# Attention and memory-augmented attention on one core: first x tiles on two DMA queues, the output bank lent to the first projections, phi's exponentials not put off, the last two head groups in turn

## The chip, the cores and the metric

The kernel runs on one core of a Trainium2 chip. The metric is the device time of one execution in microseconds (us), median of several. A profiled run is one execution with every instruction recorded; its length is called the span. Engines: TensorE (PE in the profile; PEld is its weight load), ScalarE (ACT), VectorE (DVE), GpSimd (POOL), and SyncE (SP), which here only issues DMAs. "SPq" and "ACTq" are the instruction streams of SyncE and ScalarE where they issue a DMA.

## The reference, cut to what matters

Two blocks work on their own inputs and their outputs are joined along the last axis. All inputs are bf16; S = 2048, D = 1024, 32 heads of 32.

```python
# A: plain attention, no mask
q, k, v = split(x @ wqkv)                      # 32 heads
o = softmax(q k^T / sqrt(32)) v                # per head, 2048 x 2048 scores
a = o @ wo
# B: four segments of 512 with a memory
phi = lambda t: where(t > 0, t + 1, exp(t))
for s in range(4):
    a_dot = softmax(causal(q_s k_s^T / sqrt(32))) v_s
    a_mem = (phi(q_s) M) / (phi(q_s) z + 1e-6)
    o_s = sigmoid(beta) * a_mem + (1 - sigmoid(beta)) * a_dot
    M += phi(k_s)^T v_s ;  z += sum(phi(k_s))
b = o @ wo
return concatenate([a, b], -1)
```

## The kernel before

Heads are worked four at a time, a *head group* (8 in A). A *unit* is one group with 256 queries (A) or one group with one segment (B, 32 units). A unit's scores are made in *batches*: 8 matmuls of TensorE fill two pairs of PSUM banks, and ScalarE takes the exponential of each pair (128x1024) into a ring of 20 SBUF slots. (In this kernel the results of matmuls go to PSUM banks; all else on the chip is kept in SBUF.) Later TensorE multiplies these by V and by ones ("PV") into one output bank; the slots then come free, and VectorE divides.

What makes this kernel special is that the order of instructions on each engine is not written down by hand. At build time a planner runs all these processes against *assumed* costs: each request to an engine has a cost and a priority (lower goes first), and whichever is ready in the plan is recorded next. Each engine's program is its list in that order, with semaphores between the lists. So a changed cost or priority can change orders everywhere, and a plan that misjudges costs is only noticed on the chip.

```python
def dve(n, rate=1.0):                      # assumed cost of a VectorE operation, us
    return n / rate / 960 + 0.06
PAIRS = [(0, 1), (2, 3), (4, 5)]           # score banks
OB, SB = 6, 7                              # output bank, side bank (projections, memory)
# ... cut
    def first_x(self):                     # x rows 0..511, transposed on TensorE
        # ... cut
        for t in range(4):
            yield do("SP", lambda e, t=t: e.dma_start(self.XS[:, t, :], self.A_x[0][P * t:P * t + P, :]),
                     w=[("XS", t)], cost=0.1, prio=0, tail=2.5 + 0.7 * t)
        Q.fire("x0")
        # ... 4 x (8 transposes on TensorE, copy on VectorE or ScalarE)
    def rest_x(self):                      # x rows 512..2047, transposed by the DMA
        yield ("ev", "x0")
        for c in range(1, 4):
            src = self.A_x[0][512 * c:512 * c + 512, :]
            yield do("SP", lambda e, c=c, src=src: e.dma_start(self.xA[:, :, 512 * c:512 * c + 512], src, transpose=True),
                     w=[("xA", c, t) for t in range(4)], cost=8.0, prio=1, tail=1.5)
    def b_proj(self, n):                   # K, Q, V of B's unit n
        # ... cut
            d = I - (12, 7, 2)[k]          # due so many batches ahead of the unit's scores
            while self.pos < d - self.ahead:
                yield ("ev", ("pos", d - self.ahead))
    def b_mem(self, n):                    # phi, memory read and update of unit n
        # ... cut
        yield do("ACT", lambda e: e.activation(self.E[:, k0:k1, :], KQ[:, k0:k1, :], ACTF.Exp), r=kq, w=["E"],
                 cost=0.1 + 0.427 * nk, prio=6)          # scores' exponentials have prio 0
    def batches(self):                     # order of the score batches
        # ... cut
        for a in range(2, NG * NQ):        # A's units: group after group
            u = ("A", a // NQ, a % NQ)
            out += [(u, k) for k in range(8)]
            # ... B's units strewn in
    def main(self):
        # ... cut
        self.side = Pool([SB])
        self.obank = Pool([OB])
        # ... cut
        def later():
            yield ("ev", ("xA", 3))        # then B's first weights, B's x, beta
```

## Time and profile before

Median 1254.87 us of 3 runs (1250.74 to 1260.59); the profiled run's span is 1254.4 us.

| engine | busy us | share |
|---|---|---|
| ScalarE | 1128.8 | 90% |
| TensorE | 1081.2 | 86% |
| VectorE | 482.2 | 38% |

ScalarE has the most work, and nothing in the change takes work from it. Its timeline therefore splits the span into four terms that can be compared between kernels: the *head* until the first exponential, the *idle* between the first and the end of the last exponential (the gaps over 0.15 us, which are those that the profile counts), the *work* (the rest of that stretch), and the *tail* after it. Before: 21.9 + 76.9 + 1123.8 + 31.8 = 1254.4.

The list of waits of ScalarE (engine, tile, line, who released it: total us, times, longest), kernel before:

```profile
ACT PT L826 <- PE ps L809: 70.6, 48, 6.3
ACT outsb L971 <- PE ps L965: 19.5, 7, 3.7
ACT gcol L483 <- DMA beta<-in_B_beta_dram: 6.3, 1, 6.3
```

The first line is exponentials waiting for scores (L809), the second is output copies in the tail, the last is the wait for the small vector beta.

The timeline of the head, kernel before (start us, duration us, engine, line, operation, count, and in brackets the idle before it with its releaser):

```profile
3.71 2.04 SPq L512 DMA_DIRECT2D OTA<-in_A_x_dram  x3
8.70 2.74 PE L520 MATMUL ps<-ident,OTA 128*128 128x128 bf16 x24 [3.81 <-DMA OTA<-in_A_x_dram]
12.59 3.60 PE L565 MATMUL ps<-xA,WA 128*32 128x512 bf16 x32 [1.15 <-issue]
17.08 3.61 PE L565 MATMUL ps<-xA,WA 128*32 128x512 bf16 x32 [0.89 <-DVE KA L571]
...
21.93 7.44 ACT L826 ACTIVATE WoB<-ps 128x1024 bf16<-128x1024 f32 x8 [9.44 <-PE ps L809]
50.30 0.21 ACT L483 ACTIVATE gcol<-beta 128x8 f32<-128x8 bf16 x1 [6.27 <-DMA beta<-in_B_beta_dram]
56.75 1.94 ACT L826 ACTIVATE PT<-ps 128x1024 bf16<-128x1024 f32 x2 [6.24 <-PE ps L809]
65.47 3.90 ACT L826 ACTIVATE PT<-ps 128x1024 bf16<-128x1024 f32 x4 [6.27 <-PE ps L809]
74.39 1.94 ACT L826 ACTIVATE PT<-ps 128x1024 bf16<-128x1024 f32 x2 [5.02 <-PE ps L809]
```

Tiles 1 to 3 of x land at 8.7 us, when TensorE starts to transpose them. The projections of K and Q run 32 matmuls in 3.6 us, half the rate of later ones (1.9 us; called "half rate" and "full rate" below), with 0.89 us between them for the copy out of the single side bank. After the first 24 exponentials ScalarE idles four times for 5 to 6 us.

In the middle there are six waits of 3 to 5.7 us. The chain of waits around the one that ends at 930 us, kernel before (start us, us, what):

```profile
922.67 0.70 DVE VT L571
...
923.39 3.74 DMA VB<-VT
...
927.26 0.54 PE ps L897 x16
...
929.03 0.49 DVE tB L946
...
929.57 0.40 PE ps L897 x8
929.97 0.36 PE ps L809 x8
...
930.35 1.94 ACT PT L826 x2
```

Read downward: V of a B unit is copied out, transposed by a DMA, then PV of that unit runs in two halves with VectorE's division between, and only behind these does TensorE reach the next score batch.

The end, chain of waits, kernel before:

```profile
1220.27 0.33 PE ps L809 x8
1220.60 6.16 PE ps L965 x112
...
1227.41 10.14 PE ps L965 x188
...
1241.46 5.89 PE ps L965 x107
...
1247.37 0.69 DVE outsb L971
```

After the last score batch (L809) TensorE still has 26.8 us of work to do, nearly all of it output projection (L965).

### The profile page before, as it was taken

The page shows a single profiled execution, that of the slowest core. Times are in us where ns is not written, and L with a number is a line of the kernel's source. Part 1 is how long each engine was busy: PE and PEld are TensorE (multiplying, and loading weights), DVE is VectorE, ACT ScalarE, POOL GpSimd, SP SyncE. Part 2 cuts the span into 40 slices and gives each one's busy share as a digit, 9 for nine tenths or more (in the row PEclk, how much of TensorE's full clock was granted, in tenths as well). Part 3 has the DMA queues.
Part 4 walks back from the last instruction along what each step waited for, and adds up shares of the span by engine and source line. Part 5 has one row for each costly group of instructions (what it writes and reads, how often), then busy time and mean ns, then how long its engine had stood idle before and what let it go on. Part 6 is the DMA issues. An engine that isn't in the chain of part 4 may idle for free.

```text
span 1254.4 us, 49504 instructions
## 1 busy us (share of the span) xinstructions
PE 1081.2 (86%) x23137; PEld 508.4 (41%) x23137; DVE 482.2 (38%) x1065; ACT 1128.8 (90%) x1227; POOL 125.8 (10%) x285
## 2 busy tenths in 40 slices
PE   6588989887889888888899888898888888889997
PEld 2243444443444444443444344343433444434443
DVE  1124333432434444443434444533434436324332
ACT  4469999999999899999999889999987999999981
POOL 1001000100101111111010201110111102100000
PEclk9798999999999999998999999999999999989999
DMA  8422152124212122313121223113122111120112
GB/s 167 86 53 44 36 129 52 37 45 75 52 29 56 40 53 49 57 28 73 44 61 36 48 49 61 36 40 64 38 49 60 33 38 43 32 73 32 37 45 67
DMA packets 214741, 67.23 MB, mean 54 GB/s; under 512 B 203776, under 2 KB 211968, under 8 KB 214528
## 3 DMA queue, kind: packets, MB, share of 16 engines
q1 hardware_dynamic: 214528, 63.99, 23.4%
q8 instruction: 183, 3.00, 1.0%
q14 instruction: 30, 0.25, 0.1%
HBM read 36.70 MB, written 8.39 MB: 36 GB/s over the span
## 4 chain that ended last, share of the span: by engine, by line
ACT 43%; PE 37%; DVE 13%; DMA 2%; issue 2%; SPq 1%; POOL 1%; ACTq 0%
ACT PT L826 42%; PE ps L565 12%; PE ps L897 11%; PE ps L965 7%; PE ps L809 6%; DVE Dt L919 2%; DVE Rb L922 2%; ACT E L670 1%; DVE VT L571 1%; DVE KQB L571 1%; DVE Rall L920 1%; POOL PT L835 1%; DMA beta<-in_B_beta_dram 1%; DVE OTA L926 1%; DVE amem L706 1%
## 5 line engine op out<-in xcount | busy, mean ns | idle before, releaser
L826 ACT ACTIVATE PT<-ps 128x1024 bf16<-128x1024 f32 x1168 | 1086.9, 1067 | 73.0 <-PE ps L809 70.6
L897 PE MATMUL ps<-PT,ones 128*32 128x256 bf16 (+1 forms) x4800 | 298.6, 273 | 0.0
L897 PE MATMUL ps<-PT,VA 128*32 128x256 bf16 x4032 | 256.3, 278 | 33.2 <-ACT PT L826 18.4
L565 PE MATMUL ps<-xA,WA 128*32 128x512 bf16 x3072 | 228.3, 389 | 29.0 <-DVE KQB L571 11.8
L565 PE MATMUL ps<-xB,WB 128*32 128x512 bf16 x3072 | 231.1, 387 | 25.4 <-DVE VT L571 6.7
L809 PE MATMUL ps<-QA,KA 32*128 32x256 bf16 x4096 | 205.8, 275 | 33.0 <-ACT PT L826 26.1
L835 POOL TENSOR_SCALAR_AFFINE_SELECT PT<-PT 128x256 bf16<-128x256 bf16 (+1 forms) x224 | 98.6, 441 | 952.3 <-ACT PT L826 945.9
L897 PEld LDWEIGHTS ps<-PT,VA 128*32 128x32 bf16 x4032 | 108.2, 96 | 132.5 <-ACT PT L826 90.5
L809 PEld LDWEIGHTS ps<-QA,KA 32*128 32x128 bf16 x4096 | 60.9, 92 | 214.5 <-ACT PT L826 172.1
L897 PEld LDWEIGHTS ps<-PT,ones 128*32 128x32 bf16 x4800 | 130.2, 97 | 15.3 <-issue 0.5
L565 PEld LDWEIGHTS ps<-xA,WA 128*32 128x32 bf16 x3072 | 75.5, 97 | 102.6 <-issue 48.6
L565 PEld LDWEIGHTS ps<-xB,WB 128*32 128x32 bf16 x3072 | 77.0, 97 | 94.0 <-issue 70.3
L919 DVE STREAM_TRANSPOSE Dt<-ps 128x256 f32<-128x256 f32 x128 | 57.3, 448 | 147.2 <-PE ps L897 146.5
L571 DVE CAST VT<-ps 128x512 bf16<-128x512 f32 x64 | 43.9, 686 | 139.4 <-PE ps L565 136.6
L571 DVE CAST KQB<-ps 128x512 bf16<-128x512 f32 x64 | 43.8, 685 | 137.2 <-PE ps L565 137.2
L971 DVE CAST outsb<-ps 128x512 bf16<-128x512 f32 x57 | 39.3, 690 | 114.4 <-PE ps L965 114.2
L965 PE MATMUL ps<-WoB,OTB 128*32 128x512 bf16 x1024 | 72.3, 381 | 5.0 <-DVE VT L571 1.9
L965 PE MATMUL ps<-xA,OTA 128*32 128x512 bf16 x1024 | 67.4, 388 | 1.2 <-DVE outsb L971 0.7
L922 DVE STREAM_TRANSPOSE Rb<-Rall 128x256 f32<-128x256 f32 x128 | 56.7, 443 | 3.5
L897 PE MATMUL ps<-PT,VB 128*32 128x256 bf16 (+1 forms) x768 | 46.2, 262 | 10.2 <-DVE tB L946 4.9
L809 PE MATMUL ps<-KQB 32*128 32x128 bf16 (+3 forms) x512 | 44.4, 310 | 5.2 <-ACT PT L826 4.0
L571 DVE CAST QA<-ps 128x512 bf16<-128x512 f32 x32 | 21.8, 683 | 55.1 <-PE ps L565 55.0
(67 smaller groups left out, 463.4 us busy)
## 6 DMA issues: line engine op xcount, KB each, us to landing
WB<-in_B_wk_dram SPq DMA_DIRECT2D x32, 256.0 KB, 2.8
WB<-in_B_wq_dram SPq DMA_DIRECT2D x32, 256.0 KB, 2.9
WB<-in_B_wv_dram SPq DMA_DIRECT2D x32, 256.0 KB, 3.1
out_dram<-outsb SPq DMA_DIRECT2D x64, 128.0 KB, 1.8
WA<-in_A_wqkv_dram SPq DMA_DIRECT2D x24, 256.0 KB, 2.9
WoB<-in_B_wo_dram SPq DMA_DIRECT2D x1, 2048.0 KB, 9.7
xA<-in_A_wo_dram SPq DMA_DIRECT2D x1, 2048.0 KB, 9.6
OTA<-in_A_x_dram SPq DMA_DIRECT2D x4, 256.0 KB, 4.5
```

Source lines behind the costliest of these rows:

```text
L565: ins = e.matmul(self.ps[32 * c:32 * c + 32, bank, :], W[:, i, 32 * c:32 * c + 32], x(i), start=(i == 0), stop=(i == NI - 1))
L571: return e.tensor_copy(dst, self.ps[:, bank, :])
L670: yield do("ACT", lambda e: e.activation(self.E[:, k0:k1, :], KQ[:, k0:k1, :], ACTF.Exp), r=kq, w=["E"], cost=0.1 + 0.427 * nk, prio=6)
L706: yield do("DVE", lambda e: e.scalar_tensor_tensor(self.amem[b][:, :], self.ps[:, bank, :], gA, self.mR[:, :], ALU.mult, ALU.mult), r=[("p ...
L809: ins = e.matmul(self.ps[:, bk, col:col + w], lhs(t, hs), rhs(q0, w, hs), start=True, stop=True)
L826: yield do("ACT", lambda e: e.activation(ap, self.ps[:, pr[0]:pr[1] + 1, :], ACTF.Exp, scale=SCALE), r=[("ps", bk) for bk in pr], w=keys, ...
L835: yield do("POOL", lambda e, m=m, n=n: e.affine_select(m, m, pattern=[[0, n], [1, P]], compare_op=ALU.is_ge, fill=0.0, base=0, channel_mul ...
L897: ins = e.matmul(out, l, r, start=st, stop=sp)
L919: yield do("DVE", lambda e: e.transpose(Dt[:, :], den), r=[("ps", OB)], w=[("Dt", x)], cost=dve(QU), prio=0)
L922: yield do("DVE", lambda e: e.transpose(Rb[:, :].rearrange("p (a b) -> p a b", b=32), self.spread(Rc)), r=[("Rc", ui)], w=[("Rb", x)], cos ...
L965: ins = e.matmul(self.ps[32 * c:32 * c + 32, bank, :], lhs(j)[:, 32 * c:32 * c + 32], W(j), start=(j == 0), stop=(j == NG - 1))
L971: return f(self.outsb[ob][:, :], self.ps[:, bank, :])
```

## The change

By its words: the first x tiles go out on two DMA queues; the output bank is lent to projections until the first PV; phi's exponentials get the highest priority; the last two head groups alternate by query block, so that output rows are finished steadily. The diff holds more: nine warming matmuls at the start, the transposing loads in six pieces, new planner costs, earlier due dates for B's projections, B's first loads (with beta) started at score batch 16, a longer lookahead (`ahead`: a projection may start so many batches before its due date, 12 before and 20 after), and other settings of the planner (the `par` line: B's rate, the order of PV, the dates of B's memory and output). Its core (cuts marked):

```diff
 def dve(n, rate=1.0):
-    return n / rate / 960 + 0.06
+    return n / rate * 0.00088 + (0.14 if rate == 1 else 0.07)
...  (score batch: cost 2 * N256 -> N256; exponential: 0.95 -> 0.9035; DMAs get a bandwidth model)
+    par = dict(b=(18, 14, 10), mem=-2, memM=2, span=66, rate=0.58, ahead=20, sl=4, pv=18, ob=6, lead=4, b0=1, bpos=16, wob=80)
...
+    def warm(self):
+        yield do("DVE", lambda e: e.memset(self.PT[:, 0, :], 0.0), w=[("PT", 0)], cost=0.3, prio=0)
+        # nine 128x512 matmuls of that tile
...
-            yield do("SP", lambda e, t=t: e.dma_start(self.XS[:, t, :], ...
+            Q.spawn(self.load_xs(t, "SP" if t % 2 == 0 else "ACT"))
...
-            d = I - (12, 7, 2)[k]
+            d = I - self.par['b'][k]
...
-                 cost=0.1 + 0.427 * nk, prio=6)
+                 cost=0.093 + 0.427 * nk, prio=-1)
...
+        units = [(a // NQ, a % NQ) for a in range(2, (NG - 2) * NQ)]
+        p = self.par["lead"]
+        units += [(NG - 2, q) for q in range(p)]
+        for q in range(NQ):
+            units += [(NG - 1, q)]
+            if q + p < NQ:
+                units += [(NG - 2, q + p)]
...
-        self.side = Pool([SB])
-        self.obank = Pool([OB])
+        self.side = Pool([SB, OB])
+        self.obank = Pool([])
+        self.first_pv = False
...
-        self.ahead = 12
+        self.ahead = self.par['ahead']
...
         for k in (0, 1, 2):
-            Q.spawn(self.load_WA(k, 0, 0))
+            Q.spawn(self.load_WA(k, 0, 0, "SP" if k == 0 else "ACT"))
...
         def later():
-            yield ("ev", ("xA", 3))
+            yield ("ev", ("pos", self.par["bpos"]))
```

More of the change, by code (lines that the diff above doesn't have):

```diff
@@ L26 @@
 class Op:
-    __slots__ = ("eng", "idx", "fn", "deps", "clock", "inc", "end", "waits", "dma")
+    __slots__ = ("eng", "idx", "fn", "deps", "clock", "inc", "end", "waits", "dma", "ex")
     def __init__(self, eng, idx, fn):
         self.eng, self.idx, self.fn = eng, idx, fn
-        self.deps, self.clock, self.inc, self.end, self.waits, self.dma = [], None, False, 0.0, [], None
+        self.deps, self.clock, self.inc, self.end, self.waits, self.dma, self.ex = [], None, False, 0.0, [], None, eng
 class Recorder:
@@ L66, in deps, with add @@
         return deps
-    def add(self, eng, fn, r, w, order=None):
+    def add(self, eng, fn, r, w, order=None, via="SP"):
         deps = self.deps(eng, r, w, order)
@@ L76, in add @@
             op.dma = c
+            op.ex = via
         else:
@@ L93, in resolve @@
         for op in self.all:
-            ex = "SP" if op.dma is not None else op.eng
+            ex = op.ex
             kn = known[ex]
@@ L125, in play @@
         for op in self.all:
-            if ("SP" if op.dma is not None else op.eng) != name:
+            if op.ex != name:
                 continue
@@ L155 @@
 class Req:
-    __slots__ = ("eng", "fn", "r", "w", "cost", "prio", "mode", "tail", "proc", "seq", "order")
+    __slots__ = ("eng", "fn", "r", "w", "cost", "prio", "mode", "tail", "proc", "seq", "order", "kb")
 class Pool:
@@ L178, in __init__ @@
         self.mode = None
+        self.dma_free = 0.0
         self.events = {}
@@ L277, in dispatch @@
             ready = 0.0
-            for d in self.R.deps(eng, rq.r, rq.w, rq.order):
+            for d in self.R.deps("SP" if rq.kb else eng, rq.r, rq.w, rq.order):
                 if d.end + LAT > ready and d.eng != eng:
@@ L296, in dispatch @@
         assert all(k in self.R.lastw for k in rq.r), rq.r
-        op = self.R.add(eng, rq.fn, rq.r, rq.w, rq.order)
+        op = self.R.add("SP" if rq.kb else eng, rq.fn, rq.r, rq.w, rq.order, eng)
         cost = rq.cost
@@ L305, in dispatch @@
         op.end = start + cost + rq.tail
+        if rq.kb:
+            self.dma_free = max(self.dma_free, start + min(cost, 0.6)) + rq.kb / 230
+            op.end = max(start + cost, self.dma_free) + 1.7
         self.busy[eng] += cost
@@ L321, in run, with do @@
             raise RuntimeError(f"stuck processes: {self.nproc} " + str([k for k, v in self.events.items() if v is not True]))
-def do(eng, fn, r=(), w=(), cost=0.1, prio=5, mode=None, tail=None, order=None):
+def do(eng, fn, r=(), w=(), cost=0.1, prio=5, mode=None, tail=None, order=None, kb=None):
     rq = Req()
-    rq.order = order
+    rq.order, rq.kb = order, kb
     rq.eng, rq.fn, rq.r, rq.w, rq.cost, rq.prio, rq.mode = eng, fn, list(r), list(w), cost, prio, mode
@@ L453, in pkey, with load_WA @@
         return ("WoB", i // 2) if k == 1 else ("OTA", 2 + i // 4, i % 4)
-    def load_WA(self, k, g, prio=5):
+    def load_WA(self, k, g, prio=5, via="SP"):
         col = (1024, 0, 2048)[k] + P * g
         src = self.A_wqkv.rearrange("(i p) n -> p i n", p=P)[:, :, col:col + P]
-        yield do("SP", lambda e: e.dma_start(self.WA[k][:, :, :], src), w=[("WA", k)], cost=0.1, prio=prio, tail=2.8)
+        yield do(via, lambda e: e.dma_start(self.WA[k][:, :, :], src), w=[("WA", k)], cost=0.8, prio=prio, kb=256)
         self.Q.fire(("WA", k, g))
@@ L464, in load_WB @@
         src = self.B_w[k].rearrange("(i p) n -> p i n", p=P)[:, :, P * g:P * g + P]
-        yield do("SP", lambda e: e.dma_start(self.WB[k][:, :, :], src), w=[("WB", k)], cost=0.1, prio=prio, tail=2.8)
+        yield do("SP", lambda e: e.dma_start(self.WB[k][:, :, :], src), w=[("WB", k)], cost=0.6, prio=prio, kb=256)
         self.Q.fire(("WB", k, n))
@@ L469, in load_xB @@
         src = self.B_x[0][512 * s:512 * s + 512, :]
-        yield do("SP", lambda e: e.dma_start(self.xB[:, :, :], src, transpose=True), w=["xB"], cost=8.0, prio=6, tail=2.5)
+        yield do("SP", lambda e: e.dma_start(self.xB[:, :, :], src, transpose=True), w=["xB"], cost=5.2, prio=6, kb=1024)
         self.Q.fire(("xB", s))
@@ L480, in f @@
                     return e.dma_start(self.beta[32 * h:32 * h + 32, 0:NG], src)
-            yield do("SP", f, w=[("beta", h)], cost=0.1, prio=8)
+            yield do("SP", f, w=[("beta", h)], cost=0.5, prio=8, kb=300)
         gA, gB = self.gcol[:, 0, :], self.gcol[:, 1, :]
@@ L504, in constants, with f @@
         yield pool(lambda e: e.memset(self.Mf[:, :, :], 0.0), [("Mf", g) for g in range(NG)], 1.0)
+    def warm(self):
+        yield do("DVE", lambda e: e.memset(self.PT[:, 0, :], 0.0), w=[("PT", 0)], cost=0.3, prio=0)
+        def f(e):
+            for _ in range(9):
+                ins = e.matmul(self.ps[:, SB, :], self.PT[:, 0, 0:P], self.PT[:, 0, :], start=True, stop=True)
+            return ins
+        yield do("PE", f, r=[("PT", 0)], w=[("ps", SB)], cost=3.8, prio=0, mode=FULL)
     def first_x(self):
@@ L511, in first_x @@
         for t in range(4):
-            yield do("SP", lambda e, t=t: e.dma_start(self.XS[:, t, :], self.A_x[0][P * t:P * t + P, :]),
-                     w=[("XS", t)], cost=0.1, prio=0, tail=2.5 + 0.7 * t)
-        Q.fire("x0")
+            Q.spawn(self.load_xs(t, "SP" if t % 2 == 0 else "ACT"))
         for t in range(4):
+            yield ("ev", ("XS", t))
             b = banks[t]
@@ L530, in first_x, with load_xs @@
         Q.give(self.pairs, [(banks[0], banks[1]), (banks[2], banks[3])])
+    def load_xs(self, t, via):
+        yield do(via, lambda e: e.dma_start(self.XS[:, t, :], self.A_x[0][P * t:P * t + P, :]), w=[("XS", t)], cost=0.5, prio=0, kb=256)
+        self.Q.fire(("XS", t))
+        if t == 3:
+            self.Q.fire("x0")
     def rest_x(self):
@@ L534, in rest_x, with job @@
         for c in range(1, 4):
-            src = self.A_x[0][512 * c:512 * c + 512, :]
-            yield do("SP", lambda e, c=c, src=src: e.dma_start(self.xA[:, :, 512 * c:512 * c + 512], src, transpose=True),
-                     w=[("xA", c, t) for t in range(4)], cost=8.0, prio=1, tail=1.5)
+            for t in (0, 2):
+                q0 = 512 * c + P * t
+                src = self.A_x[0][q0:q0 + 2 * P, :]
+                yield do("SP", lambda e, q0=q0, src=src: e.dma_start(self.xA[:, :, q0:q0 + 2 * P], src, transpose=True),
+                         w=[("xA", c, t), ("xA", c, t + 1)], cost=2.6, prio=1, kb=512)
             self.Q.fire(("xA", c))
-    def job(self, due, mm, keys, out, okey, wkeys, scale=None, eng="DVE", cost=None, okeys=()):
+    def job(self, due, mm, keys, out, okey, wkeys, scale=None, eng="DVE", cost=None, okeys=(), gate=None):
         Q = self.Q
@@ L546, in job @@
         for i in range(n):
+            if gate and gate[0] == i:
+                yield ("ev", gate[1])
             yield do("PE", lambda e, i=i: mm(e, i, bank), r=keys[i] + list(wkeys), w=[("ps", bank)], cost=N512,
@@ L559, in pvprio @@
     def pvprio(self):
-        return 5 if len(self.slots.items) < 6 else 14
+        return 5 if len(self.slots.items) < self.par['sl'] else self.par['pv']
     def proj(self, due, W, wkey, x, xkeys, dst, dkey, scale=None):
@@ L575, in turn @@
     def turn(self, dst, src, r, w, prio=3):
-        return do("SP", lambda e: e.dma_start(dst, src, transpose=True), r=r, w=w, cost=0.9, prio=prio, tail=2.2)
+        return do("SP", lambda e: e.dma_start(dst, src, transpose=True), r=r, w=w, cost=1.2, prio=prio, kb=128)
     def a_prep(self, g):
@@ L584, in a_prep @@
         I = self.first[("A", g, 0)]
-        span = 66
+        span = self.par['span']
         xk = lambda c: [("xA", c, t) for t in range(4)]
@@ L617, in a_prep @@
             yield do("SP", lambda e: e.dma_start(self.WoA, self.A_wo.rearrange("(j p) n -> p j n", p=P)),
-                     w=[("xA", c, t) for c in range(4) for t in range(4)], cost=0.1, prio=5, tail=10)
+                     w=[("xA", c, t) for c in range(4) for t in range(4)], cost=0.6, prio=5, kb=2048)
             Q.fire("WoA")
@@ L665, in b_mem @@
         nk = k1 - k0
-        due = self.first[("B", n)] + 4
+        due = self.first[("B", n)] + self.par["mem"]
         if n > 0:
@@ L712, in b_mem @@
             yield ("ev", ("VB", n))
-            d = due + 6
+            d = due + self.par['memM']
             bank, = yield acq(self.side, 1, d)
@@ L740, in batches @@
         acc = 0.0
-        for a in range(2, NG * NQ):
-            u = ("A", a // NQ, a % NQ)
-            out += [(u, k) for k in range(8)]
+        units = [(a // NQ, a % NQ) for a in range(2, (NG - 2) * NQ)]
[5 more added lines that the diff above has]
+                units += [(NG - 2, q + p)]
+        for i, (g, q) in enumerate(units):
+            out += [(("A", g, q), k) for k in range(8)]
+            if i < self.par["b0"]:
+                continue
             acc += self.b_rate
@@ L762, in s_all @@
         self.s_done = True
+        Q.fire("s_done")
         pr = yield acq(self.pairs, 1)
@@ L815, in s_batch @@
         else:
-            yield do("PE", lambda e: f(e, mms), r=keys, w=w, cost=2 * N256, prio=0, mode=ROW)
+            yield do("PE", lambda e: f(e, mms), r=keys, w=w, cost=N256, prio=0, mode=ROW)
         self.pos += 1
@@ L826, in exps @@
         yield do("ACT", lambda e: e.activation(ap, self.ps[:, pr[0]:pr[1] + 1, :], ACTF.Exp, scale=SCALE),
-                 r=[("ps", bk) for bk in pr], w=keys, cost=0.95, prio=0)
+                 r=[("ps", bk) for bk in pr], w=keys, cost=0.9035, prio=0)
         Q.give(self.pairs, [pr])
@@ L864, in pv_unit @@
         Q = self.Q
-        yield acq(self.obank, 1)
+        if not self.first_pv:
+            self.first_pv = True
+            yield ("ev", ("ex", u, 1))
+            yield acq(self.side, 1, -1000, lambda x: x == OB)
+        else:
+            yield acq(self.obank, 1)
         first = True
@@ L929, in finish @@
             Q.fire(("fin", "A", g, qb))
-            if g == NG - 1:
-                Q.spawn(self.out_A(qb))
             return
@@ L956, in finish, with out_rows @@
                 Q.spawn(self.out_B(s))
-    def out_rows(self, due, lhs, lkeys, W, wkey, row, col):
+    def out_rows(self, due, lhs, lkeys, W, wkey, row, col, gate=None):
         Q = self.Q
@@ L971, in out @@
             return f(self.outsb[ob][:, :], self.ps[:, bank, :])
-        yield from self.job(due, mm, lkeys, out, [("outsb", ob)], wkey, eng="any")
+        yield from self.job(due, mm, lkeys, out, [("outsb", ob)], wkey, eng="any", gate=gate)
         yield do("SP", lambda e: e.dma_start(self.out[0][row:row + P, col:col + 512], self.outsb[ob][:, :]), r=[("outsb", ob)],
-                 cost=0.1, prio=4)
+                 cost=0.5, prio=4, kb=128)
         Q.give(self.outs, [ob])
@@ L978, in out_A @@
         yield ("ev", "WoA")
+        last = qb == NQ - 1
+        for g in (NG - 2, NG - 1):
+            if last and g == NG - 1:
+                yield ("ev", "s_done")
+            else:
+                yield ("ev", ("fin", "A", g, qb))
         due = self.pos + 4
@@ L985, in out_A @@
                                            [[("OTA", j, qb // 2)] for j in range(NG)],
-                                           lambda j, ns=ns: self.WoA[:, j, ns], [("xA", 0, 0)], q0, 512 * half))
+                                           lambda j, ns=ns: self.WoA[:, j, ns], [("xA", 0, 0)], q0, 512 * half,
+                                           (NG - 1, ("fin", "A", NG - 1, qb)) if last else None))
                 due += 2
@@ L1002, in out_B @@
                                          512 * s + P * t, D + 512 * half)
-                due += 4
+                due += self.par['ob']
     def ranges(self):
@@ L1178, in load_WoB @@
     def load_WoB(self):
-        yield ("ev", ("pos", 60))
+        yield ("ev", ("pos", self.par["wob"]))
         yield do("SP", lambda e: e.dma_start(self.WoB[:, :, :], self.B_wo.rearrange("(j p) n -> p j n", p=P)),
-                 w=[("WoB", j) for j in range(NG)], cost=0.1, prio=6, tail=12)
+                 w=[("WoB", j) for j in range(NG)], cost=0.6, prio=6, kb=2048)
         self.Q.fire("WoB")
@@ L1185, in main @@
         Q = self.Q = Sched(self.R)
-        self.b_rate = 0.56
-        self.ahead = 12
+        self.b_rate = self.par['rate']
+        self.ahead = self.par['ahead']
         self.pos, self.nfin, self.s_done = 0, 0, False
@@ L1203, in main @@
         Q.spawn(self.constants())
+        Q.spawn(self.warm())
         Q.spawn(self.first_x())
         for k in (0, 1, 2):
-            Q.spawn(self.load_WA(k, 0, 0))
+            Q.spawn(self.load_WA(k, 0, 0, "SP" if k == 0 else "ACT"))
         Q.spawn(self.rest_x())
+        for qb in range(NQ):
+            Q.spawn(self.out_A(qb))
         def later():
-            yield ("ev", ("xA", 3))
+            yield ("ev", ("pos", self.par["bpos"]))
             for k in range(3):
```

## The prediction

> **What bounds the kernel now.** ScalarE, whose exponentials of the scores (one per 128x1024 pair of banks) come every 0.926 us in unbroken stretches (timeline: 33 in 30.7 us, 66 in 61.3 us). TensorE is a near second: 85 to 90% busy in every middle 100 us (table by stretches). The span of 1254.4 us splits, by ScalarE's timeline, into three:
> - head: 21.9 us until the first exponential;
> - middle: 1200.7 us from it to the end of the last one, at 1222.6 us. The waits list gives 76.9 us of idle in it (70.6 for scores, 6.3 for beta), so about 1123.8 us of work;
> - tail: 31.8 us.
>
> The change takes no work from ScalarE; it can win only in head, idle and tail.
>
> **Head, 21.9 to about 17 us.** Before, the last first-tile load lands at 8.7 us, because three weight loads are issued between tile 0 and tiles 1 to 3; the projections of K and Q then take 3.6 us each (timeline, 12.6 to 20.7 us), twice their later 1.9 us, with 0.9 us between them for the single side bank's copy. The Trainium skill ("TensorE: Matmul & The Clock Gate", part 1) says that the array starts at half rate and is released by about 3.4 us of sustained activity; 0.43 against 0.22 us per four matmuls agree. The lent bank saves the 0.9 us, tiles landing one by one 1 to 2 us. Two queues add no bandwidth ("DMA: Bandwidth & Descriptors", issuing engines are not separate DMA queues): the same seven 256 KB loads go ahead. The nine warming matmuls (3.8 us cold) end well before the projections start, at about 10 us, so I count them for half: warm 15, cold 19.
>
> **Middle idle, 76.9 to about 34 us.** 26 us lie between 44 and 82 us: ScalarE waits for beta's slow load (9.8 us), VectorE behind it, TensorE cools again. The change loads beta later. Another 27.6 us are six waits of 3 to 5.7 us (at 415, 656, 695, 720, 924 and 966 us): phi's exponential is issued only in a hole of ScalarE, and about 4 us of projections and output stand on TensorE between two score batches. Counting instructions of the new order at the traced 0.216 us (512 columns) and 0.109 us (256) per four, such stretches over 2.4 us fall from 14 to 2; but those of 1.5 to 2 us rise from 25 to 103, so the small waits (about 20 us) stay or grow.
>
> **Tail, 31.8 to about 16.5 us.** TensorE work after the last score batch falls from 26.4 to 11.2 us by the same count, as only the last query block's output waits for the end. The 6.3 us after the last copy stay.
>
> **Sum.** 17 + 1123.8 + 34 + 16.5 = 1191 us; I put 1189, 80% between 1169 and 1209. Faster by over 2%: 0.95; within: 0.04; slower: 0.01.
>
> **What would show it.** First exponential at 15 to 19 us; its first projections at 0.22 us per four if warm, 0.43 if not. ScalarE's idle before score exponentials near 30 to 35 us, with no wait over 3 us after 90 us, and no wait for beta. Last exponential about 16 us before the end, with three instead of seven ScalarE output copies after it. ScalarE's pitch stays 0.926 us.
>
> **What would make it wrong.** The 103 middling stretches adding up to waits (TensorE has under 15% to spare); VectorE, in order, holding a score-releasing copy behind phi's work; the first transposing loads, now in six pieces, landing late for K's second to fourth blocks; a lower granted TensorE clock.

## The result, and the profile after

Median 1184.07 us of 4 runs (1181.32 to 1186.94), against 1256.62 us for the kernel before: ratio 0.9426, 95% interval 0.9381 to 0.9472. A ratio is the mean time of one kernel's fast runs over that of the other's of the same rounds, so it is not quite the ratio of the medians quoted. The profiled span is 1181.5 us.

| term | before | predicted | after | change |
|---|---|---|---|---|
| head | 21.9 | 17 | 24.2 | +2.3 |
| idle between exponentials | 76.9 | 34 | 23.6 | -53.3 |
| work between first and last | 1123.8 | 1123.8 | 1116.1 | -7.7 |
| tail | 31.8 | 16.5 | 17.6 | -14.2 |
| span | 1254.4 | 1191 | 1181.5 | -72.9 |

The time came almost wholly from the idle and the tail. The head, to which the first words of the change are given, became longer.

Waits of ScalarE, kernel after:

```profile
ACT xA L544 <- PE ps L536: 9.5, 2, 8.8
ACT WoB L861 <- PE ps L844: 7.4, 1, 7.4
ACT PT L861 <- PE ps L844: 4.0, 5, 1.5
ACT PT L861 <- PE ps L844: 19.6, 31, 1.6
```

The first three lines are of the first 90 us (the first two of them lie in the head), the last is of 90 to 1130 us. No wait between exponentials is above 1.6 us any more, and there is none for beta.

The timeline of the head, kernel after:

```profile
2.07 1.93 ACTq L549 DMA_DIRECT2D OTA<-in_A_x_dram  x2
2.41 21.72 SPq L560 DMA_TRANSPOSE xA<-in_A_x_dram  x6
5.95 0.62 PE L536 MATMUL ps<-ident,OTA 128*128 128x128 bf16 x8 [0.85 <-DMA OTA<-in_A_x_dram]
13.02 2.74 PE L536 MATMUL ps<-ident,OTA 128*128 128x128 bf16 x24 [6.46 <-DMA OTA<-in_A_x_dram]
16.91 6.07 PE L591 MATMUL ps<-xA,WA 128*32 128x512 bf16 x64 [1.15 <-issue]
...
24.23 7.44 ACT L861 ACTIVATE WoB<-ps 128x1024 bf16<-128x1024 f32 x8 [7.42 <-PE ps L844]
```

Tile 0 comes at 5.9 us, where it was 3.9 before, and tile 1, on ScalarE's queue, at 13.0 us, where it was 8.7. Both projections then run without a gap (64 in 6.07 us: the lent bank), but mostly at half rate. The DMA view of the first 30 us, kernel after, says which queue was late (the last number is the median time from issue to landing):

```profile
OTA<-in_A_x_dram SPq DMA_DIRECT2D x2, 256.0 KB, 5.8
OTA<-in_A_x_dram ACTq DMA_DIRECT2D x2, 256.0 KB, 10.6
```

The same view of the kernel before:

```profile
OTA<-in_A_x_dram SPq DMA_DIRECT2D x4, 256.0 KB, 4.5
```

The end, chain of waits, kernel after:

```profile
1161.16 0.40 PE ps L844 x8
1161.56 6.61 PE ps L1003 x120
...
1169.69 2.65 PE ps L1003 x48
1172.34 0.06 DVE outsb L1009
```

After the last score batch TensorE has 10.8 us left, not 26.8.

The work fell by 7.7 us although no exponential was dropped. Two unbroken stretches from the timelines, of before and then of after:

```profile
169.60 30.69 ACT L826 ACTIVATE PT<-ps 128x1024 bf16<-128x1024 f32 x33
```

```profile
596.70 30.39 ACT L861 ACTIVATE PT<-ps 128x1024 bf16<-128x1024 f32 x33 [0.22 <-PE ps L844]
```

Of the 1183 intervals between starts of exponentials, 668 lie between 900 and 910 ns before and 805 after; the median is 904 ns in both. "Unbroken" stretches of before still held exponentials that came a few ten ns late, too little to be counted as a gap.

### The profile page after: what moved, and what is told of

It is laid out like the page before. It is cut to its first block, busy times and chain, and to the rows that moved or that the text cites. A ratio compares the mean times of both kernels' runs of the same rounds, so it can differ in the third digit from the quotient of the medians.

```text
span 1181.5 us, 49521 instructions
## 1 busy us (share of the span) xinstructions
PE 1061.9 (90%) x23146; PEld 508.2 (43%) x23146; DVE 484.6 (41%) x1070; ACT 1120.2 (95%) x1223; POOL 125.9 (11%) x285
## 4 chain that ended last, share of the span: by engine, by line
ACT 66%; PE 25%; DVE 5%; DMA 2%; issue 1%; POOL 0%; ACTq 0%; SPq 0%; DVEq 0%
ACT PT L861 64%; PE ps L591 8%; PE ps L937 7%; PE ps L844 4%; PE ps L1003 4%; ACT E L696 2%; DMA OTA<-in_A_x_dram 1%; DVE VT L597 1%; DMA VB<-VT 1%; DMA VA<-VT 1%; ACT WoB L861 1%; DVE Dt L959 1%; DVE md L722 1%; DVE Rb L962 1%; DVE QA L597 0%
## 5 line engine op out<-in xcount | busy, mean ns | idle before, releaser
L861 ACT ACTIVATE PT<-ps 128x1024 bf16<-128x1024 f32 x1168 | 1083.2, 1098 | 24.3 <-PE ps L844 23.6
L937 PE MATMUL ps<-PT,ones 128*32 128x256 bf16 (+1 forms) x4800 | 302.6, 274 | 0.0
L937 PE MATMUL ps<-PT,VA 128*32 128x256 bf16 x4032 | 258.9, 278 | 13.4 <-ACT PT L861 7.4
L844 PE MATMUL ps<-QA,KA 32*128 32x256 bf16 x4096 | 206.6, 276 | 33.1 <-ACT PT L861 26.5
L591 PE MATMUL ps<-xA,WA 128*32 128x512 bf16 x3072 | 218.2, 389 | 10.3 <-DVE md L722 2.2
L591 PE MATMUL ps<-xB,WB 128*32 128x512 bf16 x3072 | 213.8, 381 | 14.5 <-DVE QA L597 3.7
L591 PEld LDWEIGHTS ps<-xA,WA 128*32 128x32 bf16 x3072 | 73.0, 97 | 83.7 <-issue 27.0
L591 PEld LDWEIGHTS ps<-xB,WB 128*32 128x32 bf16 x3072 | 74.3, 96 | 79.5 <-issue 45.4
L1009 DVE CAST outsb<-ps 128x512 bf16<-128x512 f32 x61 | 42.0, 689 | 118.8 <-PE ps L1003 118.8
L937 PE MATMUL ps<-PT,VB 128*32 128x256 bf16 (+1 forms) x768 | 47.6, 269 | 13.5 <-DVE tB L984 3.8
L597 DVE CAST KA<-ps 128x512 bf16<-128x512 f32 x32 | 22.0, 689 | 67.3 <-PE ps L591 67.3
L844 PE MATMUL ps<-KQB 32*128 32x128 bf16 (+3 forms) x512 | 43.7, 304 | 3.8 <-ACT PT L861 2.2
```

What stands on the lines that cost most here:

```text
L591: ins = e.matmul(self.ps[32 * c:32 * c + 32, bank, :], W[:, i, 32 * c:32 * c + 32], x(i), start=(i == 0), stop=(i == NI - 1))
L597: return e.tensor_copy(dst, self.ps[:, bank, :])
L844: ins = e.matmul(self.ps[:, bk, col:col + w], lhs(t, hs), rhs(q0, w, hs), start=True, stop=True)
L861: yield do("ACT", lambda e: e.activation(ap, self.ps[:, pr[0]:pr[1] + 1, :], ACTF.Exp, scale=SCALE), r=[("ps", bk) for bk in pr], w=keys, ...
L937: ins = e.matmul(out, l, r, start=st, stop=sp)
L1009: return f(self.outsb[ob][:, :], self.ps[:, bank, :])
```

## The experiments

Twelve kernels ran, in three calls of four with 3 rounds each, all correct. Their terms, from the same reading of ScalarE's timeline ("idle" counts every gap between the first and the last exponential, so it can be a little over the waits of one line):

| run | head | idle | longest | work | tail | span | median |
|---|---|---|---|---|---|---|---|
| before | 21.9 | 76.9 | 6.3 | 1123.8 | 31.8 | 1254.4 | 1254.9 |
| after | 24.2 | 23.6 | 1.6 | 1116.1 | 17.6 | 1181.5 | 1184.1 |
| e1_hold_transposes | 17.4 | 26.5 | 2.5 | 1116.7 | 17.4 | 1178.0 | 1179.9 |
| e2_one_queue | 17.4 | 29.0 | 3.0 | 1116.8 | 17.4 | 1180.6 | 1178.1 |
| e3_tiles_first | 13.6 | 27.2 | 3.9 | 1116.5 | 17.5 | 1174.7 | 1176.4 |
| e12_tiles_first_unheld | 13.6 | 24.5 | 1.6 | 1116.9 | 17.3 | 1172.3 | 1174.1 |
| e7_no_lent_bank | 23.4 | 25.9 | 2.0 | 1116.6 | 17.7 | 1183.5 | 1186.3 |
| e5_phi_late | 25.2 | 132.7 | 13.5 | 1120.8 | 35.8 | 1314.4 | 1317.1 |
| e10_b_late | 23.2 | 28.1 | 2.5 | 1117.0 | 17.4 | 1185.7 | 1185.7 |
| e9_before_phi_now | 19.6 | 82.2 | 6.5 | 1125.1 | 26.4 | 1253.3 | 1255.6 |
| e11_before_b_early | 19.7 | 64.8 | 6.5 | 1126.1 | 25.9 | 1236.6 | 1239.2 |
| e13_before_costs | 18.6 | 133.8 | 12.3 | 1117.9 | 32.1 | 1302.5 | 1300.0 |
| e8_beta_early | 23.8 | 43.7 | 8.3 | 1116.0 | 17.9 | 1201.4 | 1207.6 |
| e6_groups_in_sequence | 24.0 | 25.3 | 1.9 | 1116.4 | 28.9 | 1194.6 | 1198.0 |

In e1, e2, e3 and e12 the planned order of work on TensorE, VectorE and ScalarE was compared with the changed kernel's before the run and is the same, apart from the DMA issues on ScalarE (the traces agree: the same work in the same order on all four engines); e7 moves some 100 rows of TensorE's order. The others are new plans, so differences of a few us between them carry no weight.

### The head: where the 2.3 us went

One caution first. Whether the two first projections run at half rate differs between runs with the same order of work. In the kernel before they took 3.60 and 3.61 us; in e9, e11 and e13, which leave the head as it is, 3.41 and 1.91, 3.60 and 1.91, 1.91 and 1.91, so their heads are 18.6 to 19.7 us and not 21.9. In the changed kernel and e5, e6, e7, e8 and e10, whose first loads are the same, heads are 23.2 to 25.2 us. So the head did become longer, by 4.0 us between the means of these four and six runs. The start of the projections is the steadier mark: 12.1 to 12.7 us in the first four runs, 16.5 to 17.7 us in the other six.

**e1_hold_transposes.** The transposing loads wait for the four tiles.

```diff
                 yield do("SP", lambda e, q0=q0, src=src: e.dma_start(self.xA[:, :, q0:q0 + 2 * P], src, transpose=True),
-                         w=[("xA", c, t), ("xA", c, t + 1)], cost=2.6, prio=1, kb=512)
+                         r=[("XS", i) for i in range(4)], w=[("xA", c, t), ("xA", c, t + 1)], cost=2.6, prio=1, kb=512)
```

> The changed kernel, with the six transposing loads of x made to wait until the four first tiles have landed. Every engine's order is unchanged. Theory (in the changed kernel the transposing loads on SP's queue share the DMA engines with the tiles on ScalarE's queue and delay those: last tile used at 13.0 us, before 8.7): last tile in by about 9 us, first exponential at 18 to 20 us instead of 24.2, span 3 to 5 us shorter than the changed kernel's if K's later blocks still come in time. Rival (ScalarE's queue is slow because two weight loads stand ahead of its tiles): tiles still at 12 to 13 us, first exponential within 1 us of 24.2.

Measured: tiles 1 to 3 at 8.6 us, first exponential at 17.4 us, span 1178.0 us (3.5 us shorter). The tiles on ScalarE's queue now took 6.0 us to land, with the same two weight loads ahead of them, so the rival falls:

```profile
OTA<-in_A_x_dram ACTq DMA_DIRECT2D x2, 256.0 KB, 6.0
```

The head is a little shorter than expected; both projections ran at full rate (64 matmuls in 3.64 us).

**e2_one_queue.** All seven first loads on SP's queue.

```diff
-            Q.spawn(self.load_xs(t, "SP" if t % 2 == 0 else "ACT"))
+            Q.spawn(self.load_xs(t, "SP"))
...
-            Q.spawn(self.load_WA(k, 0, 0, "SP" if k == 0 else "ACT"))
+            Q.spawn(self.load_WA(k, 0, 0, "SP"))
```

> The changed kernel with all first loads on SP's queue, weights ahead of tiles; the orders of TensorE, VectorE and ScalarE's work are unchanged. Theory (the second queue costs because transposing loads overtake its tiles): in one queue nothing overtakes, last tile at about 9 us, first exponential at 18 to 20 us. Rival (two queues help, and the late tiles come from the weights issued first): last tile at 12 us or later, first exponential at 23 us or later.

Measured: all tiles usable from 8.0 us, first exponential at 17.4 us, 6.9 us earlier than in the changed kernel. The projections:

```profile
12.48 3.64 PE L591 MATMUL ps<-xA,WA 128*32 128x512 bf16 x64 [1.15 <-issue]
```

They start 4.4 us earlier than the changed kernel's (12.48 against 16.91 us); that is what the second queue cost in this arrangement. The other 2.4 us are their rate (3.64 against 6.07 us), and half rate does not follow from late tiles alone: in e7 the tiles came as late and the rate was full. The span of the profiled run is only 0.9 us shorter (it is the slowest of its four runs; the medians differ by 5.9 us), because most of it was lost again by 187 us, with one wait of 3.0 us at 105 us where the changed kernel has none. There the chain shows a transposing DMA of 5.2 us; why it fell badly in that run was not followed up.

**e3_tiles_first.** As e1, and tiles ahead of weights on both queues.

```diff
-        for k in (0, 1, 2):
-            Q.spawn(self.load_WA(k, 0, 0, "SP" if k == 0 else "ACT"))
+        def weights():
+            yield ("ev", "x0")             # fired when the last tile has been issued
+            for k in (0, 1, 2):
+                Q.spawn(self.load_WA(k, 0, 0, "SP" if k == 0 else "ACT"))
+        Q.spawn(weights())
```

> As e1_hold_transposes, and on each of the two queues the two tiles are issued ahead of the weights. Seven loads of 256 KB in all, so the weights should land by 9 us as before and the tiles by 5 to 6 us. Expected: TensorE still warm from the nine warming matmuls or cold for only part of the projections, first exponential at 13 to 17 us, span 7 to 11 us shorter than the changed kernel's 1181.5. If the order of weights and tiles is of no account: as e1.

Measured: first exponential at 13.6 us, but then ScalarE waits 3.9 us for the second block of x, whose transposing load had been held; span 1174.7 us, 6.8 us shorter, just under the expected 7 to 11.

**e12_tiles_first_unheld.** As e3 without the hold (diff against e3).

```diff
-                         r=[("XS", i) for i in range(4)], w=[("xA", c, t), ("xA", c, t + 1)], cost=2.6, prio=1, kb=512)
+                         w=[("xA", c, t), ("xA", c, t + 1)], cost=2.6, prio=1, kb=512)
```

> e3_tiles_first without the hold: the four tiles at the head of both queues, then the weights, and the transposing loads not waiting for the tiles. Every engine's order of work as in the changed kernel. In e3 the tiles came in time (first exponential at 13.6 us), but ScalarE then waited 3.9 us for the transposed second block, which had been held. If that is all that is left of the head: first exponential at 13 to 16 us, no wait over 2 us behind it in the first 30 us, span 1170 to 1175. If the transposing loads delay the tiles on ScalarE's queue even when those stand first: first exponential at 17 us or later, span as e1.

Measured: first exponential at 13.6 us, next wait 1.1 us, span 1172.3 us, median 1174.08 us (four runs, 1174.0 to 1179.13; the changed kernel's four lie between 1181.32 and 1186.94). The head's timeline:

```profile
0.78 0.91 ACTq L549 DMA_DIRECT2D OTA<-in_A_x_dram  x2
5.05 2.44 PE L536 MATMUL ps<-ident,OTA 128*128 128x128 bf16 x32
8.66 3.64 PE L591 MATMUL ps<-xA,WA 128*32 128x512 bf16 x64 [1.17 <-ACT xA L544]
13.55 1.94 ACT L861 ACTIVATE WoB<-ps 128x1024 bf16<-128x1024 f32 x2 [4.98 <-PE ps L844]
16.57 5.61 ACT L861 ACTIVATE WoB<-ps 128x1024 bf16<-128x1024 f32 x6 [1.09 <-PE ps L844]
```

TensorE starts on the tiles at 5.0 us and has transposed all four at 7.5; both projections take 3.64 us together, at full rate, and 9.2 of the 10.7 us of shorter head reach the end of the run. It has the lowest median and ratio: 0.9323 of before (interval 0.9260 to 0.9387, which just touches that of the changed kernel; e3's four runs, 1174.32 to 1181.77, overlap with its own).

**e7_no_lent_bank.** The output bank is not lent.

```diff
-        self.side = Pool([SB, OB])
-        self.obank = Pool([])
-        self.first_pv = False
+        self.side = Pool([SB])
+        self.obank = Pool([OB])
+        self.first_pv = True
```

> The changed kernel with the output bank kept from the projections; only some 100 rows of TensorE's order move, ScalarE's and VectorE's are the same. If the lent bank is worth what the timeline of before shows (0.9 us between the first two projections, and again between later ones while the first 32 exponentials run): first exponential 1 us later than 24.2, waits of the first 90 us 1 to 4 us more, span 1 to 4 us more. Rival: no difference beyond 0.5 us, since projections alternate with scores anyway.

Measured: the gap of 0.89 us between the first two projections is back, yet the first exponential came at 23.4 us, 0.8 us *earlier*, because in this run the projections were at full rate (32 in 1.91 us) and in the changed kernel's mostly not. Idle is 2.3 us more, span 2.0 us, median 2.2 us more. That has the expected size, but the runs of the changed kernel alone spread over 5.6 us, so what the bank is worth is not settled.

### The idle: phi's priority, the due dates or the costs

Theory A was that the long waits come of phi being put off. Theory B was that they come of B's projections being due too late, as the chain at 922 us suggests. The traces of all runs allow a count that helps to judge: by how much the transposed V of each of B's 32 units landed before or after the first score matmul of that unit. In the kernel before it landed after it in 9 units, and the six latest (9.2 to 12.1 us) belong to the six long waits: each wait ends 3.2 to 4.4 us after such a V has landed. In the changed kernel V is late in no unit.

**e9_before_phi_now.** In the kernel before, phi's exponential is not put off, nothing else.

```diff
-                 cost=0.1 + 0.427 * nk, prio=6)
+                 cost=0.1 + 0.427 * nk, prio=-1)
```

> The kernel before with one number changed: phi's exponentials not put off. Theory A: the six waits of 3 to 5.7 us after 400 us go, idle for scores falls from 70.6 to about 45 us, span 1225 to 1235. Theory B, and the count of TensorE's order (stretches over 3.5 us stay at the same places): the waits stay, span within 8 us of 1254, but the tail may be 5 us shorter.

Measured: ratio 0.999 (0.9969 to 1.0011), median 1255.6 against 1258.0 us; the six long waits stand where they were (420, 661, 701, 725, 931, 972 us; 3.5 to 5.8 us), and V is late in the same six units. Theory A fails for the kernel before.

**e11_before_b_early.** In the kernel before, B's projections get the new due dates, nothing else.

```diff
-            d = I - (12, 7, 2)[k]
+            d = I - (18, 14, 10)[k]
```

> The kernel before with one thing changed: B's projections due 18, 14 and 10 batches ahead instead of 12, 7 and 2. Theory B: the six long waits go, idle for scores 70.6 to about 45 us, span 1222 to 1235. Theory A: they stay, span within 8 us of 1254.

Measured: ratio 0.9851 (0.9826 to 0.9876), median 1239.2 us. The six long waits are gone (two of 2.3 and 2.4 us remain after 100 us), and V is late in two units, by 2.2 us at most. Theory B holds for the kernel before. The gain is less than expected, the span just outside the range: 12 us of idle, not 25, since the waits for scores of up to 2 us grew from 39 to 62 in number and from 25.5 to 36.3 us in sum; the rest of the 17.8 us of span is a tail 5.9 us and a head 2.2 us shorter, less 2.3 us more of work.

**e10_b_late.** In the changed kernel, they get the old due dates; the planner's wait named under e5 is released too, in a slightly different way.

```diff
-    par = dict(b=(18, 14, 10), mem=-2, ...
+    par = dict(b=(12, 7, 2), mem=-2, ...
```

> The changed kernel with the old due dates of B's projections (12, 7, 2 batches ahead instead of 18, 14, 10). Theory A: idle within 8 us of 23.6, span under 1192. Theory B: the long waits come back, idle 50 us or more, span over 1205.

Measured: median 1185.7 us, idle 28.1 us. In the changed kernel the due dates alone are worth nothing that these runs can see. But this run does not refute Theory B, since it did not make V late as it was before. The lookahead stayed at 20: V's projection may start 2 + 12 = 14 batches before its unit's scores in the kernel before, 10 + 12 = 22 in e11, and 2 + 20 = 22 here. Accordingly V landed late in three units only, by 2.7, 4.6 and 7.4 us, and two waits over 2 us came back, of 2.1 and 2.5 us, behind two of these. The changed kernel with old due dates *and* old lookahead was not run.

**e5_phi_late.** In the changed kernel, phi is put off as before. A first build of this did not come off: the planner waited for a batch number past the last batch. With that wait released (which by itself leaves every order as it was) it builds.

```diff
-                 cost=0.093 + 0.427 * nk, prio=-1)
+                 cost=0.093 + 0.427 * nk, prio=6)
...
         Q.fire("s_done")
+        for i in range(self.pos + 1, self.pos + 100):
+            Q.fire(("pos", i))
...
-                while self.pos < due - self.ahead:
+                while self.pos < due - self.ahead and not self.s_done:
```

> The changed kernel with phi's exponentials put off again (and the planner's wait for a batch number that then never comes released; that release alone leaves the order as it was). Theory A (putting off phi is what makes the long waits: phi late, memory late, the next unit's V late, its output matmuls late, the ring full): eight or more waits of ScalarE over 2.5 us, idle for scores 60 us or more instead of 23.6, span 1215 to 1240. Theory B (the earlier due dates of B's projections are what removed them): idle within 8 us of 23.6, span under 1192.

Measured: median 1317.1 us, 4.75% *slower than the kernel before* (ratio 1.0475, 1.0435 to 1.0515), far outside either range. Fifteen waits over 2 us, up to 13.5 us; idle 132.7 us, and a tail of 35.8 us. The chain of waits into the longest one:

```profile
330.24 0.53 ACT E L696
...
331.78 2.41 DMA PKt<-PH
...
334.24 0.66 PE ps L745 x16
...
335.35 3.63 PE ps L591 x32
...
345.55 0.36 PE ps L846 x4
```

phi (E) is reached only now; behind it come its transposing DMA, the memory update (L745), two projections of a B unit (L591; the first is shown) that stand behind that memory update on TensorE, at half rate (32 matmuls in 3.63 us; the granted TensorE clock, as a share of full, read 0.50 from 335 to 339 us), and only then scores (L846).

This gave a third theory. With assumed costs near the real ones the plan keeps ScalarE full, so a low-priority phi finds no hole and waits until everything behind it has run dry. The old costs left holes in the plan, in which phi went out in time. (A score batch takes 0.33 us of TensorE in both traces, from its start to that of the next work; the old plan has 0.55 us for it, the new one 0.32, with 0.1 for the change of the kind of work.)

**e13_before_costs.** The kernel before with the new assumed costs of VectorE, the exponential and the score batch; phi still put off.

```diff
-    return n / rate / 960 + 0.06
+    return n / rate * 0.00088 + (0.14 if rate == 1 else 0.07)
...
-                 r=[("ps", bk) for bk in pr], w=keys, cost=0.95, prio=0)
+                 r=[("ps", bk) for bk in pr], w=keys, cost=0.9035, prio=0)
...
-            yield do("PE", lambda e: f(e, mms), r=keys, w=w, cost=2 * N256, prio=0, mode=ROW)
+            yield do("PE", lambda e: f(e, mms), r=keys, w=w, cost=N256, prio=0, mode=ROW)
```

> The kernel before with three numbers of its planner changed to the new ones: what VectorE's operations, the exponentials and a score batch are taken to cost. phi still put off. Theory (found from the run with phi put off in the changed kernel, 1317 us: with costs near the real ones the plan keeps ScalarE full, so a phi that waits for a hole waits until the ring of exponentials is blocked): waits of 5 to 13 us at five or more places, span 1290 or more, so slower than before. Rival (the new costs only make a better plan): span 1225 to 1250.

Measured: median 1300.0 us, ratio 1.0305 (1.0238 to 1.0372); waits of 4.5 to 12.3 us at nine places after 200 us. The third theory holds as far as this run goes: truer costs alone make the kernel slower. That phi is what starves is seen in the traces: in the median of B's units it went out 6 us before the unit's first scores in the kernel before, but 9 us after them here (at most 69) and 11 us after them in e5; all nine long waits end 6 to 15 us after such a late phi, seven of them after two in a row. Which of the three costs does it was not separated. The work also came down by 5.9 us to 1117.9, so most of the 7.7 us of denser exponentials seems to come with the costs.

**e8_beta_early.** In the changed kernel, `later()` again starts when the last block of x has been asked for, not at batch 16.

```diff
         def later():
-            yield ("ev", ("pos", self.par["bpos"]))
+            yield ("ev", ("xA", 3))
```

> The changed kernel with B's first loads and beta started as before, as soon as the last block of x has been asked for, not at batch 16. The 26 us of idle that before had between 44 and 82 us are put down to this in the prediction. If so: beta waited for by ScalarE (6 us), waits of 5 to 6 us between 45 and 85 us, idle 15 to 30 us more than 23.6, span 1197 to 1212. If the idle came from elsewhere (cold projections, the single side bank): idle within 6 us of 23.6.

Measured: median 1207.6 us; span 19.9 us and idle 20.1 us more than the changed kernel's (the profiled run is the fastest of four; the medians differ by 23.5 us). ScalarE waits 5.5 us for beta at 44 us, then 5.5, 8.3 and 3.2 us for scores up to 75 us. Two of these:

```profile
44.04 0.21 ACT L490 ACTIVATE gcol<-beta 128x8 f32<-128x8 bf16 x1 [5.50 <-DMA beta<-in_B_beta_dram]
68.41 3.77 ACT L861 ACTIVATE PT<-ps 128x1024 bf16<-128x1024 f32 x4 [8.28 <-PE ps L844]
```

So about 20 us of the change are the later start of B's loads.

### The tail

**e6_groups_in_sequence.** In the changed kernel, the last two groups one after the other.

```diff
-    par = dict(... ob=6, lead=4, b0=1, ...
+    par = dict(... ob=6, lead=8, b0=1, ...
```

> The changed kernel with the last two head groups one after the other, as before. TensorE's work behind the last score batch by count: 23.8 us instead of 11.2. Expected: from the last exponential to the end 29 to 31 us instead of 17.7, the rest as in the changed kernel, span 1192 to 1196.

Measured: tail 28.9 us instead of 17.6, span 1194.6 us, as expected to 0.1 us. The alternation is worth 11 us of tail, 13 of span and 14 of median, and the tail is TensorE's remaining output work.

## Why the prediction was right or wrong

**The time was right, partly by luck.** 1184.1 us lies in the range, 5 us from the number. But the head was worse than predicted by 7.2 us, and idle and work together better by 18.1 us.

**What bounds the kernel: right.** ScalarE is 95% busy after (1120.2 us), and the gain lay in idle and tail.

**Head: wrong, in direction.** The step was "Two queues add no bandwidth (...): the same seven 256 KB loads go ahead." The section quoted, "Issuing engines are not separate DMA queues" of the Trainium skill ("DMA: Bandwidth & Descriptors"), says that all queues run on the same engines and interleave. I drew from it that nothing would be gained and overlooked the other half: what one queue held back by order, two queues no longer hold back. Before, the transposing loads stood *behind* the tiles in SP's only queue. After, SP is through with its three loads at 2.4 us and starts the transposing ones, while ScalarE, behind two weights, is still issuing its two tiles (2.07 to 4.00 us). The same page ("Queues, rings and completion order") says that an engine goes round its queues packet by packet. The trace fits a sharing of the engines (10.6 us to landing on ScalarE's queue, 5.8 on SP's); the turns by packets it does not show. e1 and e2 show the overtaking from both sides, with projections that start at 12.5 us instead of 16.9, and e12 shows that the second queue does no harm once the tiles stand first.

**Half rate: the estimate "warm 15, cold 19" had the right idea but rested on tiles at about 9 us.** They came at 13 us, and the granted clock had fallen to 0.50 by 10 us; in e7, with tiles as late, the projections ran at full rate. In e12 the projections did start at full rate, and a first exponential at 13.6 us is near the 15 of the prediction. That the warming matmuls did it is not shown: no run takes them out, and e13, which has none, ran its first projections at full rate too:

```profile
12.68 1.91 PE L565 MATMUL ps<-xA,WA 128*32 128x512 bf16 x32 [1.15 <-issue]
```

**Idle: right to 10 us, and better than predicted.** The 26 us between 44 and 82 us shrank to 4.0 us up to 90 us; e8 shows that B's later loads are 20 us of it. No wait is over 1.6 us (foretold: none over 3), and the small waits came to 19.6 us after 90 us against "about 20 us". The 103 stretches of 1.5 to 2 us that the prediction feared did not add up.

**Why the six long waits went: the prediction tied them to phi being issued only in a hole, and for the kernel before that was wrong.** There phi's priority does nothing (e9); V came 9 to 12 us late in just the six units that have these waits, and earlier due dates remove both (e11). In the changed kernel V is never late. What makes it early there stays open: the due dates, the longer lookahead and the other planner settings were not taken apart (e10 takes back only the first). The new plan also needs phi first, or other long waits come (e5), and the new costs without the new priority bring such waits to the old kernel (e13). What new costs and new priority together would do in the kernel before was not run.

**Work: wrong by 7.7 us.** "ScalarE's pitch stays 0.926 us" took for a pitch what was partly small lateness; by the two stretches shown it became 0.916 (33 in 30.39 us, the last one 1.07 us long).

**Tail: right.** 16.5 predicted, 17.6 measured; the count of TensorE's remaining work gave the difference well (12.6 by count, 11.3 in e6).

## What to carry to other kernels

When a load moves to a second queue, ask what was waiting behind it in the first one and will now overtake it; put what is needed first at the head of *both* queues. In a planned schedule a low priority means "when there is a hole", so making the plan's costs truer can starve exactly the work that lived on its errors: change costs and priorities together and look for producers of long chains (here phi, then memory, then the next unit's projections). Test a bundle of changes by taking single ones out of the new kernel *and* putting them into the old one; here the two gave opposite answers for phi's priority. And check that a test really brings back the state it is meant to: e10 restored the due dates, but V hardly came later.

## What the Trainium skill lacked or had wrong

- "DMA: Bandwidth & Descriptors", "Issuing engines are not separate DMA queues": it says that several issuing engines only save issue time. It lacks the warning that a second queue also gives up order against the first. Here the first projections started 4.4 us later for it (e2 against the changed kernel); tiles took 10.6 us to land on the one queue and 5.8 on the other.
- "TensorE: Matmul & The Clock Gate", Part 1, states about 3.4 us of sustained activity for the release of half rate. Before, projections from 12.6 to 20.7 us, with one gap of 0.9 us, all ran at half rate: 8.1 us. With the same order of work it was at most 3.6 us in e9 and e11 and none in e13; in the changed kernel about 5 us (16.9 to 21.9 us), in e7 none. The page says that its window runs free and that counts vary, but 8.1 us is more than its figure suggests; these matmuls fill 32 of the array's columns each, and whether that matters was not tried.
- The same page warns in general that clock events in a trace can be unreliable; it does not name the start of a trace. In the kernel before, the column of the granted clock reads 1.00 from 10 to 20 us, while matmuls run at 0.43 us per four instead of 0.22. After, it reads 0.50 in 16 to 20 us, as the matmuls do. The durations decide.
